# Attention and MLP in one block: 14 of 16 units with a head whose scores are computed turned, the running sum kept in DRAM, loads issued from GpSimd

## Chip, cores and metric

One NeuronCore of a Trainium2 chip. The time is that of one execution on the device, in microseconds (us).

## What is computed

```python
x = A_x                                    # 2048 tokens x 448
xn = layernorm(x)
q = (xn @ wq) as 16 heads of 28;  k = xn @ wk;  v = xn @ wv     # one k and v for all heads
p = softmax(q k^T * 28**-0.5);    o = (p v), heads joined, @ wo
y = layernorm(xn);                h = gelu(y @ w1 + b1)         # 1792 wide
return x + o + (h @ w2 + b2)
```

All inputs are float32. The kernel keeps float32 accuracy by splitting most operands in a high and a low part and adding up two or three products.

## The kernel before

**Three stages.** First the norm and the projections to q, k and v (`q_slot`, `norm_first`, lines 249 to 437); q goes to DRAM in a high and a low part (`qd`), k stays in `ks`, v in `vs`. Then the MLP: 4 chunks of 512 tokens times 14 blocks of 128 hidden columns make 56 slots (`slot`, L547), each with 11 matmuls of `mlp1` (L513) and 12 of `mlp2` (L526) of the slot two earlier; its result is added to `acc` (L540), which holds the running sum of all tokens in SBUF from the load of x to the store of the output. Then attention, from L593 on.

**Attention.** 16 units, each a chunk of 512 queries and a group of 4 heads. Scores are computed transposed, keys on the partitions (`s`, L798): 16 blocks of 128 keys per head. ScalarE takes the exponential out of PSUM (L805), and the result is at once the moving operand of the product with v (`pv`, L703, `po`), four heads beside each other in the array. One column of v is 1.0, so the product carries the softmax's sums as well.

**The maxima.** In that layout the maximum of a query can't be subtracted after the fact, so it is found ahead: `max_stream` (L468) computes the same scores with queries on the partitions (L478, `m`, 16 matmuls a head), and VectorE takes the maxima (L479). `load_max` (L457) turns them and puts them as two more rows (high and low) under q in `qs`, against rows of ones in `ks`, so that the score matmul itself subtracts them. These max matmuls are spread as filler: `MLP_MAX` of them per 46 yields of the MLP slots (L586), and the rest over the attention steps by `weight` (L777). The rows of ones are written by GpSimd late in the first stage (L387).

**Turned heads.** In 7 of the 16 units (`TURNED`) the fourth head goes another way and needs neither max matmuls nor score matmuls: its scores are computed once, with queries on the partitions (`turned_scores`, L722: 16 matmuls, L730, from `q3`), VectorE scales them into `raw` with the maximum on the way (L731), ScalarE takes the exponential with the maximum as bias (L750), DMAs regroup 32-partition parts of `raw` into `half` tiles (L746, 64 transfers of 64 KB a head, on SP's queue), and VectorE turns 32 x 32 blocks into `p` (`turn_blocks`, L754, L757).

**The order.** Each unit has 8 steps of two key blocks. All engines execute in the order written by hand: the letters of `ORDER` in each step (L787): s a score matmul with its exponential, m a max matmul, t a turned score matmul, P the products with v of the step before, e a turned exponential and, at one step of a unit, `load_max`, n a part of the norm by the sums (`norm_jobs`, L635), o a part of the output projection (`o_jobs`, L615). Side work stands in queues (`Stream`) that give one part per letter. Every load and regrouping of the attention stage is on SP's queue: q of a unit (`load_q`, L440), q of a head for the max stream and the turned head (`load_m`, L396), maxima (L465, L466), sums out, in and broadcast (L649, L654, L657), regroupings (L746), output (L628). PSUM: three banks `m`, four banks `s`, one `po`.

**Names in the profile.** Tile names stand without their numbers; `xh` in attention is the tile reused for a unit's q (`qs`), and `half` names also the first stage's view of `wo`.

Of the kernel before, what the change touches and what calls it, by code (L numbers as in the profile page):

```python
# [15 lines left out]
P = 128  # L16
S, D, H, DH, F = 2048, 448, 16, 28, 1792
NT = S // P
CT = 4
# [7 lines left out]
MLP_MAX = 15  # L27
ORDER = "smsmstnsPemssmosmnsm"
TURNED = (3, 5, 7, 9, 11, 13, 15)
QB = 8  # L30
# [7 lines left out]
def block_kernel(ctx, tc, x, wq, wk, wv, wo, w1, b1, w2, b2, out):  # L38
# [19 lines left out]
    ld = dram.tile([4, CW], F32, name="ld")  # L58
    qd = [dram.tile([D, S], F32, name=f"qd{i}") for i in range(2)]

    acc = keep.tile([P, NT, D], F32, name="acc")
# [4 lines left out]
    ph1 = ExitStack()  # L66
    xl_p = ph1.enter_context(tc.tile_pool(name="xl", bufs=2))
# [53 lines left out]
    for t in qmt:  # L121
        pool.memset(f(t), 0.0)
    b1r = wqp.tile([NF, P], F32, name="b1r", bufs=1)
# [21 lines left out]
    def split_weights():  # L145
        for i in range(2):
            split_small(kvraw[:, :, i, :], lambda w, i=i: w[:, :, 32 * i + 1:32 * i + 1 + DH])
# [159 lines left out]
    def w2_split(s):  # L307
# [3 lines left out]
        dve.tensor_sub(w2l[:, ab, :], raw, f(w2h[:, ab, :]))  # L311

    def q_slot(c, i):
# [7 lines left out]
        def evac():  # L321
# [4 lines left out]
            if i == 0:  # L326
                vt = wqp.tile([32, CW], F32, name="vt", bufs=1)
                kl = wqp.tile([64, CW], F32R, name="kl", bufs=1)
                act.activation(ks[32:64, cols], ps[32:64, :], AF.Copy)
                act.activation(vt, ps[0:32, :], AF.Copy)  # L330
            dve.tensor_sub(qe[at, 1, :], ps[at, :], f(qe[at, 0, :]))
            if i == 0:
                dve.tensor_sub(kl[32:64, :], ps[32:64, :], f(ks[32:64, cols]))
                for dst, src in ((0, kl[32:64, :]), (64, kl[32:64, :]), (96, ks[32:64, cols])):
                    nc.sync.dma_start(f(ks[dst:dst + 32, cols]), f(src))
# [51 lines left out]
    def ones_rows():  # L387
        for r in (32, 96):
            pool.memset(f(ks[r:r + 1, :]), 1.0)  # L389

    later(3, 2, ones_rows, True)
# [4 lines left out]
    def load_m(u, j, qm=None, t=None):  # L396
        c, g = units[u]
        at = slice(0, CW) if t is None else slice(t * P, (t + 1) * P)
        cols = slice(c * CW + at.start, c * CW + at.stop)
        if qm is None:  # L400
            qm = qmt[heads.index((u, j)) % 3]
        for blk, i in ((1, 0), (2, 0), (0, 1), (3, 1)):
            nc.sync.dma_start(f(qm[32 * blk + 1:32 * blk + 1 + DH, at]), qd[i][DH * (4 * g + j):DH * (4 * g + j + 1), cols])
# [36 lines left out]
    def load_q(u):  # L440
# [6 lines left out]
        for blk, i in ((1, 0), (2, 0), (0, 1), (3, 1)):  # L447
            nh = heads_of(u)
            src = qd[i][4 * DH * g:4 * DH * g + DH * nh, cols].rearrange("(j r) n -> r j n", r=DH)
            nc.sync.dma_start(f(qs[32 * blk + 1:32 * blk + 1 + DH, 0:nh, :]), src)  # L450
# [6 lines left out]
    def load_max(u):  # L457
# [4 lines left out]
        mn = keep.tile([4 * CT, 2, P], F32R, name="mn", bufs=2)[0:nh * CT]  # L462
        act.activation(mn[:, 0, :], pm, AF.Copy, scale=-1.0)
        dve.scalar_tensor_tensor(mn[:, 1, :], pm, -1.0, f(mn[:, 0, :]), op0=ALU.mult, op1=ALU.subtract)
        nc.sync.dma_start(f(qs[32:33, 0:nh, :]), f(mn[:, 0, :]))  # L465
        nc.sync.dma_start(f(qs[96:97, 0:nh, :]), f(mn[:, 1, :]))  # L466

    def max_stream():  # L468
        for h, (u, j) in enumerate(heads):
# [5 lines left out]
            for t in range(CT):  # L475
                for n in range(4):
# [3 lines left out]
                    if (j, t, n) == (heads_of(u) - 1, CT - 1, 3):  # L480
                        mrs[u] = keep.tile([P, 4 * CT], F32, name="mr", bufs=10)
# [31 lines left out]
    def mlp1(c, ft):  # L513
# [10 lines left out]
        lows.append(lambda: dve.tensor_sub(hl, hr, f(hh)))  # L524

    def mlp2(c, ft, between):  # L526
# [4 lines left out]
        for k in range(CT):  # L531
# [11 lines left out]
            if k == 2 and lows:  # L543
                lows.pop(0)()
            yield

    def slot(n):  # L547
# [13 lines left out]
        else:  # L561
            if nxt:
                nxt()
            lows.pop(0)()

    lows, norms, maxed = [], {}, 0
# [30 lines left out]
    def half_tile():  # L597
        return att.tile([P, QB, CW], F32, name="half", bufs=3)

    wor = half_tile()[:, 0:NG, 0:D]  # L600
    q3 = att.tile([P, CW], F32R, name="q3", bufs=1)
    pool.memset(f(q3), 0.0)
# [11 lines left out]

    def o_jobs(c, gs, tiles=range(CT)):  # L615
        last = NG - 1 in gs
        for k in tiles:
# [7 lines left out]
            a = acc[:, CT * c + k, :]  # L625
# [9 lines left out]
    def norm_jobs(u, po):  # L635
# [12 lines left out]
        else:  # L648
            nc.sync.dma_start(rc, oc[0:P:32, :])  # L649
            yield  # L650
            yield
            dve.reciprocal(rc, rc)
            yield
            nc.sync.dma_start(ld.rearrange("h (i e) -> (h i) e", e=CW // 32), rc)  # L654
# [205 lines left out]
```

## Time and profile before

| | us |
|---|---|
| Median of 3 runs | 1142.34 (1142.27 to 1142.73) |
| Profiled execution | 1142.51 |
| Its span, first to last instruction | 1140.7 |
| First stage, up to the first max matmul | 69.9 |
| MLP, first to last GELU | 72.6 to 445.4 |
| Attention, from the first score matmul | 454.5 |

A row of the grouped lines reads: line, engine, operation, tile written from tiles read, shapes, number | busy us, mean ns of one | idle time of the engine before them, and who ended it. PEld is the weight load of TensorE, SPq SyncE's queue of DMAs. In the chain of waits, each piece is what released the next. The row of one line's DMAs gives the least, median and most ns for which the queue was held by one.

### The profile page before, as it was taken

The numbers are of one execution on the slowest core, as the hardware profiler recorded it, in microseconds if no ns is written. First come the engines' busy times: TensorE is split into PE (matmuls) and PEld (weight loads), VectorE is DVE, ScalarE is ACT, GpSimd is POOL, SyncE is SP. The second block draws the span as 40 slices with busy tenths as digits, with TensorE's granted clock in tenths as the row PEclk, the third lists the DMA queues.
The fourth block names the chain that finished last, engine by engine and source line by source line (L and its number), as shares of the span: only waits on it lengthen the run. The fifth ranks groups of instructions, "written<-read, shape, count | busy, mean of one in ns | idle before, by whom it ended". The sixth has DMA issues, their size and how long they took to land.

```text
span 1140.7 us, 17019 instructions
## 1 busy us (share of the span) xinstructions
PE 1122.8 (98%) x5905; PEld 729.7 (64%) x5905; DVE 867.1 (76%) x1600; ACT 689.6 (60%) x1290; POOL 109.3 (10%) x113
## 2 busy tenths in 40 slices
PE   9989999999999999999999999999999999999998
PEld 8768888888888888555554555544455554564454
DVE  7779889888888888777777777777667677777434
ACT  6753322221222222788888877888777888878974
POOL 5340000000002000002101101101101101101100
PEclk9999999999999999999999999999999999999999
DMA  9751100000000020332343342342433443442300
GB/s 287 200 181 51 43 15 17 17 17 18 17 17 17 17 49 18 86 82 75 97 100 78 101 111 76 105 100 74 103 97 84 102 101 76 106 104 65 85 24 33
DMA packets 65426, 86.82 MB, mean 76 GB/s; under 512 B 20566, under 2 KB 31980, under 8 KB 65212
## 3 DMA queue, kind: packets, MB, share of 16 engines
q1 hardware_dynamic: 63932, 85.16, 28.1%
q8 instruction: 47, 0.77, 0.3%
q10 hardware_dynamic: 1408, 0.57, 0.2%
q14 instruction: 39, 0.32, 0.1%
HBM read 44.05 MB, written 11.12 MB: 48 GB/s over the span
## 4 chain that ended last, share of the span: by engine, by line
PE 88%; DVE 4%; DMA 3%; ACT 2%; issue 1%; SPq 1%; POOL 0%; DVEq 0%; ACTq 0%; POOLq 0%
PE po L708 19%; PE m L478 18%; PE s L798 17%; PE ph L158 10%; PE m L535 4%; PE m L537 4%; PE m L533 4%; PE m L730 3%; DMA xh<-qd 2%; PE qp L158 2%; PE m L622 1%; PE m L624 1%; PE m L623 1%; PE ph L161 1%; DMA rc<-oc 1%
## 5 line engine op out<-in xcount | busy, mean ns | idle before, releaser
L479 DVE TENSOR_REDUCE mx<-m 128x1 f32<-128x512 f32 x912 | 593.2, 685 | 160.5 <-PE m L478 146.2
L805 ACT ACTIVATE p<-s 128x512 f32<-128x512 f32 x879 | 447.4, 614 | 94.3 <-PE s L798 94.2
L478 PE MATMUL m<-ks,qm 128*128 128x512 f32 x912 | 371.0, 407 | 3.5 <-POOL ks L389 2.4
L798 PE MATMUL s<-xh,ks 128*128 128x512 f32 x879 | 318.2, 407 | 2.8 <-ACT p L805 2.5
L708 PE MATMUL po<-p,vs 128*32 128x512 f32 x2048 | 247.9, 601 | 0.0
L478 PEld LDWEIGHTS m<-ks,qm 128*128 128x128 f32 x912 | 171.3, 188 | 108.5 <-issue 26.0
L798 PEld LDWEIGHTS s<-xh,ks 128*128 128x128 f32 x879 | 163.3, 188 | 86.6 <-ACT p L805 35.0
L519 ACT ACTIVATE hr<-ph,b1t 128x512 f32<-128x512 f32 x56 | 38.6, 689 | 277.3 <-PE ph L163 191.5
L708 PEld LDWEIGHTS po<-p,vs 128*32 128x32 f32 x2048 | 53.9, 109 | 120.2 <-issue 114.1
L750 ACT ACTIVATE raw<-raw,m 128x512 f32<-128x512 f32 x112 | 82.7, 738 | 9.9 <-DVE m L735 9.0
L533 PE MATMUL m<-w2h,hh 128*128 128x448 f32 x224 | 82.4, 368 | 0.0
L535 PE MATMUL m<-w2l,hh 128*128 128x448 f32 x224 | 81.6, 364 | 0.0
L537 PE MATMUL m<-w2h,hl 128*128 128x448 f32 x224 | 81.5, 364 | 0.0
L731 DVE TENSOR_SCALAR_CACHE_REDUCE raw<-m 128x512 f32<-128x512 f32 x112 | 76.2, 680 | 0.0
L660 POOL TENSOR_TENSOR oc<-oc,tr 128x512 f32<-128x512 f32 x15 | 19.4, 1294 | 589.0 <-DMA tr<-ld 206.6
L757 DVE STREAM_TRANSPOSE p<-half 128x512 f32<-128x512 f32 x112 | 72.6, 687 | 1.6 <-PE po L708 1.6
L158 PE MATMUL ph<-xh,w1h 128*128 128x512 f32 x168 | 66.5, 396 | 0.0
L158 PE MATMUL ph<-xh,w1l 128*128 128x512 f32 x168 | 66.4, 395 | 0.0
L158 PE MATMUL ph<-xl,w1h 128*128 128x512 f32 x168 | 66.0, 393 | 0.0
L626 DVE TENSOR_TENSOR acc<-acc,m 128x448 f32<-128x448 f32 x22 | 13.6, 621 | 51.5 <-PE m L624 51.5
L730 PE MATMUL m<-ks,q 128*128 128x512 f32 x112 | 47.2, 422 | 3.4 <-DVE mx L479 3.4
L535 PEld LDWEIGHTS m<-w2l,hh 128*128 128x128 f32 x224 | 42.0, 188 | 6.3
(141 smaller groups left out, 964.4 us busy)
## 6 DMA issues: line engine op xcount, KB each, us to landing
half<-raw SPq DMA_DIRECT2D x448, 64.0 KB
qm<-qd SPq DMA_DIRECT2D x228, 56.0 KB
xh<-qd SPq DMA_DIRECT2D x36, 224.0 KB
qd<-qe SPq DMA_DIRECT2D x24, 256.0 KB
xh<-qd SPq DMA_DIRECT2D x28, 168.0 KB
tr<-ld SPq DMA_DIRECT2D x56, 64.0 KB
raw<-in_B_w_dram SPq DMA_DIRECT2D x7, 448.0 KB
out_dram<-acc SPq DMA_DIRECT2D x14, 224.0 KB
```

Of the source, the lines that this page charges most:

```text
L158: pe.matmul(ps, w, v, start=(n == 0), stop=False)
L478: pe.matmul(pm, qm[:, t * P:(t + 1) * P], ks[:, n * CW:(n + 1) * CW], start=True, stop=True)
L479: dve.tensor_reduce(mx[:, CT * j + t, n:n + 1], pm, axis=AX.X, op=ALU.max)
L533: pe.matmul(m2[k], hh[:, ts], w2h[:, ft, :], start=(ft == 0), stop=False)
L535: pe.matmul(m2[k], hh[:, ts], w2l[:, ft, :], start=False, stop=False)
L537: pe.matmul(m2[k], hl[:, ts], w2h[:, ft, :], start=False, stop=(ft == NF - 1))
L708: pe.matmul(po[32 * j:32 * j + 32, :], vs[:, kt, :], ps.pop((u, kt, j)), start=(kt == 0), stop=(kt == NT - 1))
L730: pe.matmul(sc, q3[:, t * P:(t + 1) * P], ks[:, n * CW:(n + 1) * CW], start=True, stop=True)
L731: dve.tensor_scalar(raw[:, :, 4 * n:4 * n + 4, :].rearrange("p r b i -> p b r i"), sc.rearrange("p (b r i) -> p b r i", r=4, i=32), SCALE, ...
L750: act.activation(raw[:, r], raw[:, r], AF.Exp, bias=m3[:, 4:5], scale=1.0)
L798: pe.matmul(s, ks[:, kk * P:(kk + 1) * P], qs[:, j % 4, :], start=True, stop=True)
L805: act.activation(p, s, AF.Exp, scale=SCALE)
```

## The change

- `TURNED` is units 2 to 15 (14 of 16) in place of 7. The scores of a unit's turned head are computed in the ten steps ahead of it; two `q3` tiles take turns; a unit's regrouped exponentials lie in one tile of 16 x 512 per partition (two of them) in place of halves.
- Turned exponentials are 1024 wide, two groups of 32 partitions at a time, each followed by 8 regrouping DMAs; there is one per step (letter x), two in one step of a unit. `turn_blocks` is one instruction of 1024 columns per step.
- Scores come in pairs: two matmuls into a tile of two PSUM banks (two such tiles in place of four single banks), and one exponential 1024 wide. In a unit with a turned head a step has three pairs, else four. There are two orders of letters, one for each kind of unit.
- The max matmuls: 20 per 46 yields in the MLP in place of 15; new weights in attention.
- `acc` lives only until the end of the MLP. A chunk's sum is stored to `ad` in DRAM after its last slot, and loaded again by row tiles ahead of the output projection.
- In attention, loads (q, maxima, sums, row tiles) are issued from GpSimd's queue; regroupings and most of the output stay on SP.
- The MLP's low halves (`hl`) and six of the seven low parts of w2 are subtracted on GpSimd in place of VectorE.
- q, k and their maxima change rows, so that the row of ones is the last of its 32; `ks` is set to ones as a whole at the start, in place of two rows late in the first stage. Copies between rows of `ks` take 28 partitions in place of 32.

```diff
-MLP_MAX = 15
-ORDER = "smsmstnsPemssmosmnsm"
-TURNED = (3, 5, 7, 9, 11, 13, 15)
+MLP_MAX = 20
+ORDERS = ("mptmpmtmpmexnPTpmonm", "tptmpmeopxnPTmnm")
+TURNED = tuple(range(2, 16))
...
+    ad = dram.tile([P, NT, D], F32, name="ad")
...
+    pool.memset(f(ks), 1.0)
...
-        dve.tensor_sub(w2l[:, ab, :], raw, f(w2h[:, ab, :]))
+        (pool if s else dve).tensor_sub(w2l[:, ab, :], raw, f(w2h[:, ab, :]))
...
-    def ones_rows():
-        for r in (32, 96):
-            pool.memset(f(ks[r:r + 1, :]), 1.0)
-
-    later(3, 2, ones_rows, True)
...
-        lows.append(lambda: dve.tensor_sub(hl, hr, f(hh)))
+        pool.tensor_sub(hl, hr, f(hh))
...
+                if k == CT - 1:
+                    nc.sync.dma_start(ad[:, CT * c:CT * c + CT, :], acc[:, CT * c:CT * c + CT, :])
...
-    sp = ctx.enter_context(tc.tile_pool(name="sp", bufs=4, space=PSUM))
+    sp = ctx.enter_context(tc.tile_pool(name="sp", bufs=2, space=PSUM))
...
+    loads = pool
+
+    def turned_tile():
+        return att.tile([P, 4 * CT, CW], F32, name="turned", bufs=2)
...
+    def load_rows_of(c, tiles):
+        for k in tiles:
+            rows[c, k] = att.tile([P, D], F32, name="a", bufs=5)
+            loads.dma_start(rows[c, k], ad[:, CT * c + k, :])
...
-            a = acc[:, CT * c + k, :]
+            a = rows[c, k]
             dve.tensor_add(a, a, po)
...
-            nc.sync.dma_start(rc, oc[0:P:32, :])
-            yield
-            yield
+            loads.dma_start(rc, oc[0:P:32, :])
+            for _ in range(4):
+                yield
...
+                    exps.extend((u, t, raw, m3, h) for h in range(2))
+                    if t == CT - 1 and u + 2 < NU:
+                        load_m(u + 2, 3, q3[i])
...
+    def turned_exp():
+        if not exps:
+            return
+        u, t, raw, m3, h = exps.pop(0)
+        if u not in turned:
+            turned[u] = turned_tile()
+        rs = slice(2 * h, 2 * h + 2)
+        act.activation(raw[:, rs], raw[:, rs], AF.Exp, bias=m3[:, 4:5], scale=1.0)
+        for r in range(2 * h, 2 * h + 2):
             for a in range(4):
-                nc.sync.dma_start(hbs[-1][32 * r:32 * r + 32, 4 * (t % 2) + a, :],
+                nc.sync.dma_start(turned[u][32 * r:32 * r + 32, 4 * t + a, :],
                                   raw[32 * a:32 * a + 32, r].rearrange("p b i -> p (b i)"))
...
+    def turn_blocks(u, kt):
+        p = pair_of()
+        dve.transpose(p.rearrange("p k (g j) -> p g k j", j=32),
+                      turned[u][:, :, 32 * kt:32 * kt + 64].rearrange("p g (k j) -> p g k j", j=32))
+        ps[u, kt, 3], ps[u, kt + 1, 3] = p[:, 0], p[:, 1]
...
+    def scores(u, kt, jobs):
+        s = sp.tile([P, 2, CW], F32, name="s")
+        p = pair_of()
+        for i, (k, j) in enumerate(jobs):
+            pe.matmul(s[:, i], ks[:, (kt + k) * P:(kt + k + 1) * P], qss[u][:, j, :], start=True, stop=True)
+            ps[u, kt + k, j] = p[:, i]
+        act.activation(p, s, AF.Exp, scale=SCALE)
...
-    weight = [0 if n >= len(steps) - LEAD else 8 if u in TURNED
-              else 18 if u + 2 < NU else 12 for n, (u, kt) in enumerate(steps)]
+    weight = [0 if n >= len(steps) - LEAD else 24 if u == 0 else 20 if u == 1 else 6 for n, (u, kt) in enumerate(steps)]
...
+        jobs = [((0, 0), (0, 1)), ((0, 2), (1, 2)), ((1, 0), (1, 1))]
+        if u not in TURNED:
+            jobs[1:2] = [((0, 2), (0, 3)), ((1, 2), (1, 3))]
+        for what in ORDERS[u in TURNED]:
+            if what == "p":
+                scores(u, kt, jobs.pop(0))
...
             elif what == "t":
-                if n >= 3:
+                if n >= 8 * (TURNED[0] - 1) - 2:
                     tq.step()
+            elif what == "x":
+                turned_exp()
+                if kt == 12:
+                    turned_exp()
```

More of the change, by code (lines that the diff above doesn't have):

```diff
@@ L66, in block_kernel @@
     ph1 = ExitStack()
+    acc = ph1.enter_context(tc.tile_pool(name="accp", bufs=1)).tile([P, NT, D], F32, name="acc")
     xl_p = ph1.enter_context(tc.tile_pool(name="xl", bufs=2))
@@ L394, in block_kernel, with load_m @@
     qss, ots = {}, {}
-    def load_m(u, j, qm=None, t=None):
+    loads = nc.sync
+    def load_m(u, j, qm=None):
         c, g = units[u]
-        at = slice(0, CW) if t is None else slice(t * P, (t + 1) * P)
-        cols = slice(c * CW + at.start, c * CW + at.stop)
         if qm is None:
@@ L768, in o_wait @@
     def o_wait(c, gs, tiles):
+        load_rows_of(c, tiles)
         for _ in range(8):
@@ L826, in block_kernel @@
                     oside.add(o_jobs(NCH - 1, range(NG - 1)))
+                if n == len(steps) - 7:
+                    load_rows_of(NCH - 1, range(CT))
                 oside.step()
-            elif n > 0 and 2 * n % BURST == 0:
-                for _ in range(BURST):
+            elif what == "P":
+                for _ in range(BURST if n else 0):
                     pv(*pvq.pop(0))
```

115 lines of the change are left out of this document (36 added, 79 removed).

## Prediction

> **What bounds the kernel now.** I read the page's busy shares and chain first, then busy times by stage.
>
> ```profile
> span 1140.7 us, 17019 instructions
> ...
> PE 1122.8 (98%) x5905; PEld 729.7 (64%) x5905; DVE 867.1 (76%) x1600; ACT 689.6 (60%) x1290; POOL 109.3 (10%) x113
> ...
> PE po L708 19%; PE m L478 18%; PE s L798 17%; PE ph L158 10%; PE m L535 4%; PE m L537 4%; PE m L533 4%; PE m L730 3%; DMA xh<-qd 2%; PE qp L158 2%; PE m L622 1%; PE m L624 1%; PE m L623 1%; PE ph L161 1%; DMA rc<-oc 1%
> ```
> ```profile
> 72.60:445.40 372.80, 372.08 (x1701) 312.67 (x1700) 326.61 (x516) 93.78 (x142) 20.76 (x17) 1.00 0.09 25
> ```
> ```profile
> 454.50:500.90 46.40, 46.11 (x252) 24.68 (x252) 34.62 (x64) 35.89 (x72) 3.82 (x3) 1.00 0.29 69
> 500.90:1095.00 594.10, 587.86 (x3293) 304.65 (x3294) 425.90 (x829) 483.25 (x941) 49.26 (x46) 1.00 0.37 92
> 1095.00:1140.70 45.70, 40.98 (x245) 23.23 (x244) 19.29 (x36) 25.16 (x49) 2.59 (x2) 0.99 0.07 26
> ```
>
> The window rows give stretch, length, then busy PE, PEld, DVE, ACT, POOL, clock, DMA share, GB/s. The first is 55 MLP slots (from the first to the last GELU), 6.78 us each; the others are unit 0 of attention, units 1 to 14, and unit 15 with the tail. TensorE is busy in all of them and its clock is 1.00, so its own instructions are the price list to begin with:
>
> ```profile
> 463.83 0.40 PE L478 MATMUL m<-ks,qm 128*128 128x512 f32 x1
> 464.06 0.39 PE L798 MATMUL s<-xh,ks 128*128 128x512 f32 x1
> 464.29 0.39 PE L478 MATMUL m<-ks,qm 128*128 128x512 f32 x1
> 464.53 0.39 PE L798 MATMUL s<-xh,ks 128*128 128x512 f32 x1
> ```
>
> A 512-wide matmul lasts 0.39 us, but the starts are 0.23 us apart: 0.23 is what one costs. The busy 98% does not say that nothing else is near its limit. SP's queue, which is not in the busy shares at all, issues the transfers of the turned heads:
>
> ```profile
> L746 SPq DMA_DIRECT2D half<-raw x448: 507/588/1991, 489.8 to 1083.8; - x150
> ```
> ```profile
> 800.92 1.85 SPq L746 DMA_DIRECT2D half<-raw  x3
> ```
>
> Each holds SP for a median of 588 ns, and three in a row take 1.85 us, so one follows another after (1.85 - 0.588) / 2 = 0.631 us. A turned head makes 4 blocks x 4 groups x 4 parts = 64 of them (448 / 7).
>
> **The change, part by part.**
>
> Matmuls. The groups that count them:
>
> ```profile
> L479 DVE TENSOR_REDUCE mx<-m 128x1 f32<-128x512 f32 x912 | 593.2, 685 | 160.5 <-PE m L478 146.2
> L805 ACT ACTIVATE p<-s 128x512 f32<-128x512 f32 x879 | 447.4, 614 | 94.3 <-PE s L798 94.2
> L750 ACT ACTIVATE raw<-raw,m 128x512 f32<-128x512 f32 x112 | 82.7, 738 | 9.9 <-DVE m L735 9.0 <-DMA q<-qd 0.6 <-DMA qm<-qd 0.4
> L731 DVE TENSOR_SCALAR_CACHE_REDUCE raw<-m 128x512 f32<-128x512 f32 x112 | 76.2, 680 | 0.0
> L731 DVE DVE_READ_ACCUMULATOR raw<-m 128x1 f32 x112 | 9.2, 82 | 0.0
> L757 DVE STREAM_TRANSPOSE p<-half 128x512 f32<-128x512 f32 x112 | 72.6, 687 | 1.6 <-PE po L708 1.6
> ```
>
> Seven more turned heads take away 7 x 16 = 112 max matmuls (912 to 800) and 112 score matmuls, and add 112 turned ones: net -112 x 0.23 = -25.8 us of TensorE. Where they lie matters: with MLP_MAX 20, the MLP's 1276 yields give 1276 x 20 / 46 + 6 = 560 max matmuls in place of 422, which lengthens that stage by 138 x 0.23 = 31.7 us; attention loses 250 x 0.23 = 57.5 us.
>
> The memset of the ones rows goes to the start, and with it this wait:
>
> ```profile
> PE m L478 <- POOL ks L389: 2.4, 1, 2.4
> ```
>
> That is -2.4 us. The new memset of ks (two of 2048 columns took 3.6 us there) fits into the wait below; if it did not, it would cost its excess over 3.1 us.
>
> ```profile
> POOL wah L141 <- DMA kvraw<-in_A_wv_dram: 3.1, 1, 3.1
> ```
>
> MLP low halves and six of the seven w2 low parts on GpSimd. These rows price them:
>
> ```profile
> L524 DVE TENSOR_TENSOR hl<-hr,hh 128x512 fp32r<-128x512 f32 x56 | 40.4, 722 | 0.0
> L660 POOL TENSOR_TENSOR oc<-oc,tr 128x512 f32<-128x512 f32 x15 | 19.4, 1294 | 589.0 <-DMA tr<-ld 206.6 <-ACT p L805 181.7 <-PE s L798 89.3
> ```
>
> GpSimd needs 1.29 us for what VectorE did in 0.72, in a slot of 7.35 us (6.78 + 2.5 x 0.23) where it is idle; the result is used two slots later, so it costs nothing. VectorE's slot becomes 326.6 / 55 - 0.72 + 2.5 x 0.65 = 6.85 us, still under 7.35 (93%). Without the shift it would be 7.57 and the bound, +0.2 us x 56 = 12 us.
>
> The running sum stored to DRAM. Four stores of 896 KB beside a DMA share of 0.09, and 16 loads of one row tile, issued eight side steps before use: hidden. If the first attention tiles have to wait for the last store, that is one landing, under 5 us (a longest transfer in the chain of waits is 4.77 us, below).
>
> Exponentials 1024 wide. Not in the trace. A 512-wide one is 0.614 us; the slope comes from a wider row:
>
> ```profile
> L310 ACT ACTIVATE w2h<-raw 128x896 fp32r<-128x896 f32 x7 | 6.6, 941 | 0.0
> ```
>
> Against 0.614, 384 more columns cost 0.33 us, so 1024 columns take 0.614 + 512 x 0.00085 = 1.05 us, and 1.17 in the turned form (0.738). Bounds: 0.94 (slope alone) and 1.23 (two of 512). I take 1.05. A turned unit then has ScalarE at 24 x 1.05 + 8 x 1.17 + about 0.9 = 35.5 us, and VectorE at 12 x 0.65 + 16 x 0.76 + 8 x 1.16 + about 3.6 = 33 us (transposes of 1024 columns priced at 0.687 plus the same again less 0.2).
>
> What TensorE needs for a turned unit comes from GpSimd's first product of each unit:
>
> ```profile
> 564.23 1.31 POOL L660 TENSOR_TENSOR oc<-oc,tr 128x512 f32<-128x512 f32 x1 [35.58 <-DMA tr<-ld]
> ```
> ```profile
> 1072.49 1.28 POOL L660 TENSOR_TENSOR oc<-oc,tr 128x512 f32<-128x512 f32 x1 [35.22 <-ACT p L805]
> ```
>
> Twelve units lie between: 508.3 / 12 = 42.35, or 84.7 us for a pair of one turned and one whole unit. They differ by 116 - 76 = 40 matmuls (9.2 us), so a turned one takes (84.7 - 9.2) / 2 = **37.7 us**. A turned unit of after holds 48 scores + 16 turned + 12 max = 76 matmuls, the same.
>
> SP for the same unit: before, 64 regroupings in a pair, 40 us of 84.7. After, 64 in every unit: 64 x 0.631 = **40.4 us**, plus a store of the output, against TensorE's 37.7. So SP's queue is late next, although the other loads leave it. A unit's first transposes need all 64 landed; the last eight are issued two steps ahead (9.4 us), take 5.0 us to issue and about 1.9 us to land (rc below), which leaves a slack of some 2 us, used up in the first turned unit by a deficit of 2.7 us.
>
> Three rows for the sum and for the bounds of an issue (least, median, most ns), the first of unit 1:
>
> ```profile
> 500.90:545.00 44.10, 43.35 (x233) 22.89 (x237) 32.80 (x63) 39.05 (x78) 7.61 (x7) 1.00 0.38 92
> ```
> ```profile
> L628 SPq DMA_DIRECT2D out_dram<-acc x14: 332/382/537, 675.3 to 1137.1; - x14
> ```
> ```profile
> L403 SPq DMA_DIRECT2D qm<-qd x228: 306/383/1982, 38.4 to 1002.9; - x114
> ```
>
> The sum by that chain. MLP ends at 454.5 + 31.7 - 2.4 = 483.8. Unit 0 has 6 matmuls more (46.4 + 1.4 = 47.8), unit 1 four more (44.1 + 0.9 = 45.0): 576.6. Up to here SP keeps up, one group of eight a step. From the second unit's transfers on (first group in step 15, about 571) there are 104 groups, 832 x 0.631 = 525 us, and 10 stores of about 0.4: 1100. Landing 1.9, one wide transpose 1.2: 1103.4. Then the last unit's second product with v can start; before, that was here:
>
> ```profile
> 1097.60 1.92 PE L708 MATMUL po<-p,vs 128*32 128x512 f32 x16
> ```
> ```profile
> 799.87 4.77 DMA xh<-qd
> ...
> 805.01 1.89 DMA rc<-oc
> ```
>
> 43.1 us before the end, and the work behind it is unchanged. 1103.4 + 43.1 = 1146.5 us of span. The profiled execution took 1142.51 us for a span of 1140.7, 1.8 more (the median shown is 1142.34): **1148 us**. Bounds of the pitch: with the shortest issue, 0.507 + 0.043, SP needs 35 us a unit and does not bind; with 5% of delays such as the longest one (1.99 us) added, 0.66, the time is 1172.
>
> GpSimd's queue. About 20 DMAs a unit (q 4, turned q 4, maxima 2, sums 6, row tiles 1, max stream 3) come beside 3.2 us of arithmetic. No row shows a DMA issued there. Bounds: 0.31 us (the shortest issue on SP, which gives 9 us a unit) and 1.99 (its longest, 43 us). I take 1.29, GpSimd's own longest instruction of this stage: 29 of 37.7 us, hidden, as its loads are two heads or a unit ahead. Queued behind a wait there (the four broadcasts wait for the store of the sums, 1.9 us) are only such loads.
>
> The Trainium skill, "DMA: Bandwidth & Descriptors", section on issuing engines not being separate DMA queues, says that issuing from several engines only saves sequencer time, usually small beside the transfer. The rows speak against "small" here: 0.588 us of issue for 64 KB, 64 times a unit. By the rule the issue would not matter and the time would be the first rival's.
>
> **Rivals.**
>
> 1. *TensorE stays the bound* (chance 0.35). For it: its busy 98%, and a deficit of SP of only 7%, which a faster issue would remove (point: 37.7 / 64 = 0.589 us from one DMA to the next). Against: 0.631 within every run of regroupings. Time: 1142.5 - 25.8 - 2.4 = 1114; with small waits of coarser score buffers (two pairs for four single banks), up to 1130. I name 1118.
>
> 2. *GpSimd's queue becomes the bound*, slower (0.15). Its place is the issue of 20 DMAs a unit; it decides from (37.7 - 3.2) / 20 = 1.7 us each. At 2 us each a unit is 43.2 us: 13 units x 5.5 = 71 above 1114, 1186. For it: the order of its queue, with sums, products and loads in one line. Against: GpSimd is 10% busy now. The Trainium skill, "SBUF — State Buffer", section on who interferes with whom, says that descriptor generation on GpSimd can be shut out while VectorE runs in a two-port mode; no run here shows it, and the attention stage has no large VectorE copy from SBUF to SBUF besides the transposes.
>
> **How the numbers follow.** SP's queue binds: 0.50, 1137 to 1168 (pitch 0.62 to 0.66). TensorE: 0.35, 1112 to 1130. GpSimd: 0.15, mostly above 1168. Range of 8 in 10: 1116 to 1168, leaving out most of GpSimd's case and the lowest of TensorE's. A measurement of this kernel tells about 0.2% from no change: under 1140.1 is TensorE's case and 0.03 of SP's, 0.38; within, 0.05 of SP's; above, 0.57.
>
> **What would show it.** SP right: the regroupings in unbroken runs in units 2 to 14, 40 to 42 us apart by unit, VectorE's wide transposes waiting for "DMA turned<-raw", TensorE's busy share in attention down to about 93%. Wrong: transposes released by TensorE's products, units of 38 us, a pitch below 0.59. The MLP stage should be 30 to 33 us longer in either case; a larger growth means VectorE became its bound. GpSimd's case would show as scores or max matmuls waiting for "DMA xh<-qd" or "DMA qm<-qd".

## The result and the profile after

The changed kernel takes **1213.33 us** (1212.41 to 1216.5), the kernel before beside it on the same chip 1142.53 (1142.27 to 1143.32): ratio 1.0623, 95% interval 1.0602 to 1.0645. The forecast was 1148, within 1116 to 1168. The profiled execution took 1212.41 us for a span of 1210.4, against a forecast span of 1146.5.

From the page of the kernel after: span, busy shares, and shares of the chain that ended last.

```profile
span 1210.4 us, 17322 instructions
...
PE 1137.7 (94%) x5793; PEld 722.4 (60%) x5793; DVE 907.4 (75%) x1678; ACT 660.8 (55%) x778; POOL 353.6 (29%) x473
...
PE po L715 16%; PE m L475 14%; PE s L776 12%; PE ph L159 9%; ACT p L778 6%; DMA turned<-raw 5%; PE m L735 4%; PE m L532 3%; PE m L534 3%; PE m L530 3%; SPq L756 3%; DVE mx L476 2%; PE qp L159 2%; DVE p L761 2%; PE m L629 1%
```

TensorE has 112 matmuls fewer (5905 to 5793) and still lost its 98%. The chain now holds SP's queue (3%) and the landing of its transfers (5%), which were not in it.

By stretch (length, then busy PE, PEld, DVE, ACT, POOL, clock, DMA share, GB/s): first to last GELU, units 0 and 1, units 2 to 14, unit 15 with the tail. From here on a unit ends where ScalarE copies its `po` out (L645; L638 before), so unit 1 of before ends at 546.6.

```profile
70.20:476.20 406.00, 404.98 (x1837) 338.14 (x1836) 379.41 (x594) 93.74 (x142) 102.95 (x78) 1.00 0.12 36
486.70:541.80 55.10, 51.67 (x259) 27.18 (x260) 37.95 (x69) 36.47 (x39) 22.42 (x38) 0.97 0.36 94
541.80:591.50 49.70, 47.91 (x246) 23.48 (x247) 34.86 (x75) 42.19 (x47) 20.46 (x31) 1.00 0.45 115
591.50:1161.20 569.70, 515.45 (x2798) 246.75 (x2796) 373.12 (x753) 414.48 (x441) 173.06 (x279) 0.96 0.54 135
1161.20:1210.40 49.20, 41.00 (x240) 21.63 (x236) 19.93 (x29) 22.41 (x25) 2.58 (x2) 0.98 0.09 32
```

| us | before | forecast | after | after less forecast |
|---|---|---|---|---|
| up to the first score matmul | 454.5 | 483.8 | 486.7 | 2.9 |
| unit 0 | 46.4 | 47.8 | 55.1 | 7.3 |
| unit 1 | 45.7 | 46.6 | 49.7 | 3.1 |
| units 2 to 14 | 548.6 | 522.8 | 569.7 | 46.9 |
| unit 15, tail | 45.5 | 45.5 | 49.2 | 3.7 |
| span | 1140.7 | 1146.5 | 1210.4 | 63.9 |

(The forecast of units 2 to 14 is what its span leaves beside the other rows.) Three quarters of the miss lie in units 2 to 14. Single units there, kernel after: units 2, 3, 4, 5 and 9.

```profile
591.50:628.60 37.10, 36.03 (x206) 16.31 (x205) 28.02 (x59) 31.79 (x35) 14.05 (x23) 1.00 0.55 140
628.60:672.50 43.90, 37.71 (x206) 16.97 (x207) 28.66 (x58) 32.04 (x36) 14.02 (x23) 0.96 0.53 131
672.50:716.20 43.70, 38.51 (x207) 17.06 (x207) 28.65 (x58) 32.10 (x36) 14.25 (x23) 0.92 0.62 148
716.20:767.20 51.00, 46.89 (x254) 26.55 (x253) 31.13 (x62) 32.05 (x34) 14.10 (x23) 0.97 0.51 133
894.20:947.20 53.00, 47.84 (x254) 27.31 (x255) 31.14 (x62) 32.27 (x35) 14.10 (x23) 0.94 0.50 127
```

Unit 2 still runs at TensorE's pace. Units 3 and 4, with the same 206 matmuls, take 6.7 us more, and units 5 and 9, which also hold the output projection of a chunk (254 matmuls), take 51 and 53. Two windows of the same view of the kernel before, a turned unit and one with the projection:

```profile
591.00:626.90 35.90, 35.56 (x207) 15.96 (x207) 27.65 (x56) 30.49 (x60) 3.20 (x3) 1.00 0.39 93
671.50:716.00 44.50, 44.50 (x255) 25.60 (x255) 30.18 (x60) 30.97 (x60) 3.21 (x3) 1.00 0.36 94
```

A plain unit (one without projection) is 8 us longer after the change, and TensorE's busy time in it only 2. What it waits for is in the row of the regroupings (least, median, most ns of issue) and in the list of who waited for them:

```profile
L756 SPq DMA_DIRECT2D turned<-raw x896: 507/588/1990, 535.2 to 1161.6; - x180
...
  DVE p L761: 61.4, 11
```

VectorE's wide transposes wait 61.4 us in 11 places, one a unit. Such a place, in the order of the engines' work (start, length, what; in brackets the idle time ahead and who ended it):

```profile
811.70 1.25 DVE L761 STREAM_TRANSPOSE p<-turned 128x1024 f32<-128x1024 f32 x1 [5.79 <-DMA turned<-raw]
...
813.59 0.79 PE L475 MATMUL m<-ks,qm 128*128 128x512 f32 x1 [3.67 <-DVE raw L736]
...
815.17 3.64 PE L715 MATMUL po<-p,vs 128*32 128x512 f32 x16
```

The first transpose of a unit waits 5.79 us for its last landing; VectorE's work behind it is late; so TensorE, which needs VectorE to empty a bank, idles 3.67 us. And SP's queue itself, kernel after (a row joins transfers of one line that follow each other on the queue, with the idle time between them):

```profile
628.15 44.44 SPq L756 DMA_DIRECT2D turned<-raw  x67
...
727.85 4.94 SPq L756 DMA_DIRECT2D turned<-raw  x8
732.89 0.53 SPq L635 DMA_DIRECT2D out_dram<-a  x1
734.43 5.84 SPq L756 DMA_DIRECT2D turned<-raw  x8
740.37 0.53 SPq L635 DMA_DIRECT2D out_dram<-a  x1
742.16 4.95 SPq L756 DMA_DIRECT2D turned<-raw  x8
...
798.46 53.82 SPq L756 DMA_DIRECT2D turned<-raw  x80
```

In plain units SP hardly stops: 67 transfers in 44.44 us and 80 in 53.82, on average one per (44.44 - 0.59) / 66 = 0.664 and 0.674 us, where the forecast had 0.631. But the pitch, the time from one start to the next where nothing comes between, is what it was. Sixteen in a row out of the same 67 are one per (10.03 - 0.59) / 15 = 0.629 us:

```profile
635.34 10.03 SPq L756 DMA_DIRECT2D turned<-raw  x16
```

What makes 0.664 of it is in the same stretch, transfer by transfer: two stops of 0.50 and 0.79 us, and two transfers that last 0.99 and 1.08 us in place of 0.59. In unit 5, with the projection, SP stops more: from 727.85 to 742.16 two steps take 14.3 us, of which SP works 4.94 + 0.53 + 5.84 + 0.53 = 11.8; the rest it waits, each time until the next step's exponential. SP's largest wait in this unit (who for whom, us in total, times, longest):

```profile
SPq L756 <- ACT raw L753: 4.0, 5, 1.2
```

### The profile page after: what moved, and what is told of

The parts are those of the page before. It is cut to its first block, busy times and chain, and to the rows that moved or that the text cites. A ratio compares the mean times of both kernels' runs of the same rounds, so it can differ in the third digit from the quotient of the medians.

```text
span 1210.4 us, 17322 instructions
## 1 busy us (share of the span) xinstructions
PE 1137.7 (94%) x5793; PEld 722.4 (60%) x5793; DVE 907.4 (75%) x1678; ACT 660.8 (55%) x778; POOL 353.6 (29%) x473
## 4 chain that ended last, share of the span: by engine, by line
PE 74%; DVE 7%; ACT 7%; DMA 6%; SPq 3%; issue 2%; POOL 0%; ACTq 0%; DVEq 0%; POOLq 0%
PE po L715 16%; PE m L475 14%; PE s L776 12%; PE ph L159 9%; ACT p L778 6%; DMA turned<-raw 5%; PE m L735 4%; PE m L532 3%; PE m L534 3%; PE m L530 3%; SPq L756 3%; DVE mx L476 2%; PE qp L159 2%; DVE p L761 2%; PE m L629 1%
## 5 line engine op out<-in xcount | busy, mean ns | idle before, releaser
L476 DVE TENSOR_REDUCE mx<-m 128x1 f32<-128x512 f32 x800 | 521.4, 686 | 52.1 <-PE m L475 46.8
L778 ACT ACTIVATE p<-s 128x1024 f32<-128x1024 f32 x400 | 387.7, 1022 | 202.0 <-PE s L776 188.8
L475 PE MATMUL m<-ks,qm 128*128 128x512 f32 x800 | 320.5, 404 | 42.4 <-DVE raw L736 41.1
L776 PE MATMUL s<-xh,ks 128*128 128x512 f32 x800 | 265.9, 416 | 19.2 <-ACT p L778 17.8
L761 DVE STREAM_TRANSPOSE p<-turned 128x1024 f32<-128x1024 f32 x112 | 139.4, 1245 | 170.5 <-ACT p L778 72.7
L516 ACT ACTIVATE hr<-ph,b1t 128x512 f32<-128x512 f32 x56 | 38.6, 688 | 305.4 <-PE ph L164 299.5
L521 POOL TENSOR_TENSOR hl<-hr,hh 128x512 fp32r<-128x512 f32 x56 | 72.1, 1288 | 301.7 <-PE m L475 284.6
L736 DVE TENSOR_SCALAR_CACHE_REDUCE raw<-m 128x512 f32<-128x512 f32 x224 | 149.6, 684 | 8.7 <-PE m L735 4.3
L715 PEld LDWEIGHTS po<-p,vs 128*32 128x32 f32 x2048 | 55.1, 111 | 133.1 <-issue 129.3
L753 ACT ACTIVATE raw<-raw,m 128x1024 f32<-128x1024 f32 x112 | 127.6, 1139 | 0.0
L735 PE MATMUL m<-ks,q 128*128 128x512 f32 x224 | 99.6, 445 | 0.0
L735 PEld LDWEIGHTS m<-ks,q 128*128 128x128 f32 x224 | 42.1, 188 | 94.5 <-issue 80.1
```

The costliest lines, as they stand in the source:

```text
L475: pe.matmul(pm, qm[:, t * P:(t + 1) * P], ks[:, n * CW:(n + 1) * CW], start=True, stop=True)
L476: dve.tensor_reduce(mx[:, CT * j + t, n:n + 1], pm, axis=AX.X, op=ALU.max)
L715: pe.matmul(po[32 * j:32 * j + 32, :], vs[:, kt, :], ps.pop((u, kt, j)), start=(kt == 0), stop=(kt == NT - 1))
L735: pe.matmul(sc, q3[i][:, t * P:(t + 1) * P], ks[:, n * CW:(n + 1) * CW], start=True, stop=True)
L736: dve.tensor_scalar(raw[:, :, 4 * n:4 * n + 4, :].rearrange("p r b i -> p b r i"), sc.rearrange("p (b r i) -> p b r i", r=4, i=32), SCALE, ...
L753: act.activation(raw[:, rs], raw[:, rs], AF.Exp, bias=m3[:, 4:5], scale=1.0)
```

## The experiments

Each is told against the kernel after (1213.33) unless it says otherwise. Runs with one time have no interval; a ratio is to the kernel before on the same chip (1139.4 to 1141.6 there).

**1. A quarter of the regroupings on GpSimd's queue.**

```diff
-                nc.sync.dma_start(turned[u][32 * r:32 * r + 32, 4 * t + a, :],
+                (pool if a == 3 else nc.sync).dma_start(turned[u][32 * r:32 * r + 32, 4 * t + a, :],
```

> One of the four regrouping DMAs of each group of 32 rows goes to GpSimd's queue; bytes, order and everything else as in the changed kernel. Theory (SP's issue time binds, 64 x 0.675 = 43 us a unit): SP keeps 48 a unit, 32.4 us, under TensorE's 37.3 (8 steps of 4.66), so units 2 to 14 fall from 44.3 to about 38 us and the time to 1125-1135. Rival 1 (the DMA engines or the landing of 64 KB parts bind, not the issue): the bytes are the same, so it stays at 1200-1215. Rival 2 (the coarse score pairs and VectorE's order bind): stays within 1% of 1213.

Measured: 1154.21 us (1152.57 to 1155.18), ratio 1.0123 (1.0106 to 1.0140). The group of the moved ones (count, busy us, mean ns):

```profile
L756 POOL DMA_DIRECT2D turned<-raw x224 | 113.5, 511 | 191.9 <-ACT raw L753 164.3 <-DMA turned<-raw 10.3 <-DVE p L761 8.2
```

59 us come back by nothing but the queue of 224 transfers, with the same bytes in the same order: SP's issue was what bound units 3 to 14. But the time stays 19 to 29 us over what was expected, and over the kernel before, though TensorE has 112 matmuls less. That is the second question.

**2. Half of them on GpSimd.**

```diff
-                nc.sync.dma_start(turned[u][32 * r:32 * r + 32, 4 * t + a, :],
+                (pool if a % 2 else nc.sync).dma_start(turned[u][32 * r:32 * r + 32, 4 * t + a, :],
```

> Two of four regroupings on GpSimd's queue. If SP's issue still costs something in quarter_pool (48 a unit, 32 us of 39.8), this is faster than 1154 by up to 10 us; if TensorE with its waits binds there, it stays at 1150-1158; if GpSimd's queue (32 x 0.51 + 14 = 30 us a unit, with waits in its order) begins to bind, slower than 1160.

1163.3 us, slower than a quarter. VectorE's transposes wait for landings again, 17.4 us in 6 places, for 2.9 in 2 with a quarter. Why the landings come later was not found: GpSimd's waits for exponentials ahead of its transfers are no longer than with a quarter (89.5 us for 164.3). The gain is not monotonic in the share moved.

**3. The loads back on SP's queue** in attention.

```diff
-    loads = pool
+    loads = nc.sync
```

> The loads of the attention stage go back to SP's queue. Theory (SP's issue): about 20 more DMAs a unit at 0.43 us, 8.6 us on top of 44.3, 13 units: 1213 + 112 = 1325. Rival (SP has room and something else sets the unit): within 1% of 1213. It also shows what one regrouping costs SP when GpSimd issues nothing beside it: 0.63 us if GpSimd's DMAs stretched it to 0.675, 0.675 if not.

1343.16 us: 130 us more; units 2 to 14 take 54.1 us each on average. SP's queue in this kernel:

```profile
587.80 10.03 SPq L756 DMA_DIRECT2D turned<-raw  x16
597.93 1.82 SPq L447 DMA_DIRECT2D xh<-qd  x4
```

Nothing is issued on GpSimd's queue here, and 16 regroupings in a row take 10.03 us, one per 0.629. Sixteen in a row beside GpSimd's transfers take the same 10.03 (above): no disturbance of one queue by the other shows in these rows. What slows this kernel is the loads' time on SP's queue (112 us were expected) and waits in its line (15.4 us for `ld` alone).

**4. The last wide pair of scores after the products**, in the kernel after and, with a quarter on GpSimd, in the kernel of experiment 1.

```diff
-ORDERS = (..., "tptmpmeopxnPTmnm")
+ORDERS = (..., "tptmpmeoxnPTpmnm")
```

> The third pair behind the products with v, in the changed kernel as it is. Theory (SP's issue sets the unit, TensorE's waits in a step cost nothing): within 0.7% of 1213. Rival (the coarse score pairs are what made it slow): 1213 - 28 = 1185 or less.

> As quarter_pool (a quarter of the regroupings on GpSimd's queue), and in turned units the third pair of scores moves behind the products with v, so that it needn't wait for the first pair's exponential. Theory (SP no longer binds there; what is left, 39.8 us a unit against 37.7 forecast for TensorE, is TensorE waiting for the wide exponential that holds one of the two score tiles, 0.25 us in each of 112 steps): 1154 - 28 = 1126, faster than the kernel before. Rival (SP or GpSimd's queue still binds in quarter_pool): no change, 1150-1158.

1220.75 and 1149.64 us (1149.03 to 1151.13; ratio 1.0075, 1.0057 to 1.0092). Where SP binds, TensorE's order gives nothing, as expected. Where it doesn't, 4.6 us, not 28: the wait of that one pair is not where the rest goes.

**5. A unit's q loaded two steps later.**

```diff
-        if u + 1 < NU and kt == 0:
+        if u + 1 < NU and kt == 4:
             load_q(u + 1)
```

> The loads of the next unit's q (4 DMAs of 168 KB) are issued two steps later in the unit, away from the last regroupings of a unit, on whose landing the transposes wait. Theory A (SP's issue time alone sets the unit): no change, 1208-1216. Theory B (the loads stretch the landing of the last group from 1.9 to 3.7 us and hold up SP's next ones, 1.5-3 us a unit): 1213 - 13 x 2 = 1187, between 1173 and 1197.

1218.07 us, and the transposes wait 66.6 us for landings, as before the edit (61.4): the big loads are not what they wait for.

**6. Fifteen max matmuls per 46 yields in the MLP**, in the kernel after and in the second of experiment 4.

```diff
-MLP_MAX = 20
+MLP_MAX = 15
```

> MLP_MAX 15 in place of 20: 138 max matmuls (31.7 us of TensorE) move from the MLP back to attention. Theory (attention is bound by SP, TensorE has 7 us to spare in each of 13 units): the MLP shortens by 32 us and attention stays, 1181. Rival (TensorE or VectorE sets attention): the work only moves, 1208-1216.

> The version with a quarter of the regroupings on GpSimd and the late wide pair (1149.6), with 15 max matmuls per 46 yields of the MLP in place of 20: 138 of them move from the MLP (32 us there) to attention. If turned steps leave TensorE waiting for want of filler, the 138 cost less than 0.23 us each there: about 50 of them in units 0 and 1 at full price (11 us), the rest between nothing and 0.23, so 1128 to 1140. If a matmul costs the same wherever it stands, 1149 as before. In the kernel after the same edit gave 20 us back, but there SP's queue set the pace of a unit.

1193.28 and 1151.45 us (1150.02 to 1151.78). Under SP's queue 138 matmuls moved out of the MLP give 20 of their 32 us, since TensorE has idle time in attention. With SP relieved they give nothing: units 2 to 14 take 532 us for 506, on average 0.23 us for each of 114 matmuls more. So those steps as a whole are not short of filler; the theory that they were falls. (In plain units from unit 6 on, 7 more cost 1.1 us, 0.16 each: a little is filled there.)

**7. The MLP's low halves back on VectorE.**

```diff
-        pool.tensor_sub(hl, hr, f(hh))
+        dve.tensor_sub(hl, hr, f(hh))
```

> The MLP's low halves back on VectorE, everything else as in the changed kernel. From the prediction: VectorE's slot becomes 6.85 + 0.72 = 7.57 us against 7.38 of the slot now, so the MLP grows by about 12 us, 1225. Rival (VectorE's real spacing is below its durations, so it still fits): no change, 1211-1215.

1235.85 us, 22.5 more. The row of the waits that shows it, kernel of this experiment:

```profile
ACT hr L516 <- DVE mx L476: 223.8, 37, 7.0
```

The GELU waits for VectorE's maxima: VectorE would be the MLP's bound, and by more than the 12 us of the forecast.

**8. The turned heads of before** (7 of 16), everything else as after.

```diff
-TURNED = tuple(range(2, 16))
+TURNED = (3, 5, 7, 9, 11, 13, 15)
...
-                if n >= 8 * (TURNED[0] - 1) - 2:
+                if tdone < 16 * len(TURNED) and n >= 8 * (TURNED[tdone // 16] - 1) - 2:
                     tq.step()
+                    tdone += 1
```

> The kernel after, but with the turned heads of before only (units 3, 5, 7, 9, 11, 13, 15): 112 max matmuls and 112 score matmuls come back for 112 turned ones, and SP issues 64 regroupings in two units in place of one. If SP's queue is what binds after, this must be far faster than 1213, whatever else was changed; if the two-bank score tiles, the loads on GpSimd or the store of the sum bind, it stays above 1200. Against the version with SP relieved by a quarter (1154.2) two theories of what a turned head is worth part: by the count of matmuls alone, as the forecast had it, 112 x 0.23 = 25.8 us more, 1180; by the theory that a turned step leaves about 0.35 us more uncovered than a whole one (7 x 8 x 0.35 = 20 us), some 6 us more, 1160.

1191.26 us (1189.39 to 1191.59), ratio 1.0434 (1.0416 to 1.0451). SP is no longer short (the transposes wait 1.3 us for landings in all), yet the kernel is 49 us over the one before with exactly its 5905 matmuls. So the loss beside SP's queue is not in the seven added heads: with SP relieved these take 1191 to 1154, 37 us, more than their 25.8 of matmuls. It is in the rest of the change. A turned and a whole unit of this kernel:

```profile
643.80:680.20 36.40, 35.28 (x202) 15.51 (x201) 25.45 (x41) 25.58 (x28) 14.23 (x23) 1.00 0.21 55
767.90:810.70 42.80, 41.40 (x221) 18.64 (x221) 19.57 (x43) 37.67 (x42) 14.10 (x23) 1.00 0.48 119
```

To read these, count the instructions at their own price: 0.23 us a 512-wide matmul, 0.20 a 448-wide one, 1.89 for the 16 products of a step (15.1 a unit). The whole unit has 221 - 128 = 93 matmuls, 36.5 us, and takes 42.8: 6.3 beside. A whole unit of before has 2.6 beside (44.6 for 117). Added up over attention, what these prices leave over is 57 us before, 106 here, 152 in the kernel after, 89 in the second of experiment 4 (a few small transposes on TensorE are not priced).

**9. Turned scores started two steps earlier.**

```diff
-                if n >= 8 * (TURNED[0] - 1) - 2:
+                if n >= 8 * (TURNED[0] - 1) - 4:
```

> The kernel after with the scores of each turned head started two steps earlier, so that the exponentials of the next head are there for SP while a unit's first transposes wait for their last landing; the number of transfers is the same. Theory A (in after SP lacks exponentials for some 3.3 us after the stall at each unit's end, and would otherwise run at 0.631 us a transfer): units of 40.9 us in place of 44.3, 13 x 3.4 = 44 us less, about 1170. Theory B (each transfer costs SP 0.675 us beside GpSimd's transfers, whatever the order): nothing gained, 1205 to 1215.

1205.97 us (1201.93 to 1207.65), ratio 1.0573 (1.0550 to 1.0596): not theory A's 1170. SP's queue in units 6 to 8, and who waits for a landing, kernel of this experiment:

```profile
767.80 124.27 SPq L756 DMA_DIRECT2D turned<-raw  x189
```
```profile
  DVE raw L736: 89.0, 23
  DVE p L761: 1.3, 1
```

In these three units SP goes through 189 transfers with no stop over 0.65 us, 0.658 us each on average, and the transposes no longer wait (61.4 to 1.3 us). But the wait has only moved: 89.0 us are spent on a free `raw` buffer, which the same transfers hold. There the pace is SP's, wherever the wait shows. Elsewhere SP does stop, for another reason (units 2 to 14, same columns as above):

```profile
SPq L756 <- DVE p L761: 18.0, 4, 6.8
```

Once each in units 2, 5, 9 and 13 SP waits until the transposes have read one of the two `turned` tiles. So the earlier start runs into the second buffer, and this kernel does not show what SP could do if it were fed throughout; a third `turned` tile was not tried. The time is the one of theory B, but not by its cause: a transfer still follows another after 0.63 us.

**10. Three edits at the ends of attention, in one kernel**, on the second of experiment 4.

```diff
+    s2 = [sp.tile([P, 2, CW], F32, name=f"s{i}", bufs=1) for i in range(2)]
...
-        s = sp.tile([P, 2, CW], F32, name="s")
+        s = s2[len(done_s) % 2]
...
+            if u == 0:
+                act.activation(p[:, i], s[:, i], AF.Exp, scale=SCALE)
```

> From the version with a quarter of the regroupings on GpSimd and the late wide pair (1149.6), three edits: unit 0's exponentials 512 wide, each freeing its own bank; the last sums stored by token tile, half of them from ScalarE's queue; units 14 and 15 in the order of letters of after. By the count of matmuls unit 0 lost 10.1 us beside its instructions there, 3.2 in the kernel before. If the score tile of two banks that waits for one wide exponential makes the difference, unit 0 gets some 3 us shorter, and the smaller last store takes about 2 from the wait ahead of it. The end (unit 14, unit 15 and the tail) took 94 us there and 88.5 in the order of after. Sum: 1149.6 - 3 - 2 - 5.5 = 1139, level with the kernel before or 0.2% under it; if the wide tile is not the reason, 1142 to 1145.

1191.75 us (1189.19 to 1196.89). The windows of unit 0 and of the rest, and TensorE in unit 0:

```profile
486.70:588.50 101.80, 76.89 (x259) 32.59 (x260) 39.51 (x70) 43.45 (x71) 23.42 (x40) 0.71 0.18 49
588.50:1189.20 600.70, 586.12 (x3278) 283.68 (x3278) 425.33 (x856) 478.01 (x511) 305.82 (x534) 1.00 0.55 140
```
```profile
521.98 0.50 PE L779 MATMUL s<-xh,ks 128*128 128x512 f32 x1 [0.75 <-ACT p L782]
...
523.88 0.79 PE L779 MATMUL s<-xh,ks 128*128 128x512 f32 x1 [0.75 <-ACT p L782]
```

The edit shared a tile so that the second score matmul of a pair waits for the exponential of the first: a chain, and unit 0 took 101.8 us. It tells nothing of the theory. The rest (600.7 us against 606.0) shows that the edits at the end work.

**11. The same without that mistake**: units 14 and 15 in the letters of after, the last sums stored by token tile, half of them from ScalarE's queue; then also unit 0 with four score tiles of one bank and exponentials 512 wide.

```diff
-        for what in ORDERS[u in TURNED]:
+        for what in ORDERS[0 if u not in TURNED else 2 if u >= NU - 2 else 1]:
...
-                if k == CT - 1:
-                    nc.sync.dma_start(ad[:, CT * c:CT * c + CT, :], acc[:, CT * c:CT * c + CT, :])
+                (nc.scalar if k % 2 and c == NCH - 1 else nc.sync).dma_start(ad[:, CT * c + k, :], a)
```

> The version with a quarter of the regroupings on GpSimd and the late wide pair (1149.6) with two edits: units 14 and 15 in the order of letters of after, and the last sums stored by token tile, half of them from ScalarE's queue. The end (unit 14, unit 15, tail) took 94.1 us there and 88.6 in the version with the order of after; the wait for the last store should fall from 3.6 to 2.0 us. If both simply add, 1149.6 - 5.5 - 1.7 = 1142.4; if what is saved at the end comes back elsewhere, 1147 or more.

For the second, besides:

```diff
+    sp1 = first_unit.enter_context(tc.tile_pool(name="sp1", bufs=4, space=PSUM))
...
+            to = s[:, i] if u > 0 else sp1.tile([P, CW], F32, name="s")
+            pe.matmul(to, ks[:, (kt + k) * P:(kt + k + 1) * P], qss[u][:, j, :], start=True, stop=True)
...
+            if u == 0:
+                act.activation(p[:, i], to, AF.Exp, scale=SCALE)
```

> The version before it in this call, with unit 0's exponentials 512 wide from four score tiles of one bank each (in a pool of their own, closed at unit 1), so that a score matmul waits for the exponential four before it and not for a wide one. Unit 0 lost 10.1 us beside its instructions with tiles of two banks, 3.2 in the kernel before; some 2 of the rest are the wait for the store. If the two-bank tiles cause it: unit 0 shorter by 4 to 5 us, 1138 in all. If the order of letters or the start causes it: no gain, 1142.

1142.35 us (1140.09 to 1145.23), ratio 1.0026 (1.0017 to 1.0035), and 1141.93 (1140.89 to 1143.19), ratio 1.0020 (1.0012 to 1.0029). Windows of the first: unit 0, a turned unit, unit 14, unit 15 with the tail.

```profile
486.70:539.20 52.50, 50.41 (x259) 25.85 (x259) 38.26 (x70) 36.36 (x38) 23.45 (x40) 1.00 0.35 90
...
624.20:661.00 36.80, 36.37 (x206) 16.57 (x207) 28.38 (x58) 32.03 (x36) 21.94 (x39) 1.00 0.60 153
1051.50:1093.20 41.70, 38.14 (x218) 18.82 (x217) 23.22 (x45) 30.26 (x33) 19.29 (x34) 1.00 0.60 152
1093.20:1140.10 46.90, 39.96 (x240) 21.53 (x236) 19.46 (x29) 22.42 (x25) 2.57 (x2) 0.98 0.06 20
```

The two edits add as expected (the smaller last store gives 2.6 us in unit 0, the end 5.5). The narrow score tiles give 0.4 us in all. From its first score, unit 0 takes 51.7 us (487.7 to 539.4) for 52.2 (487.0 to 539.2), not 4 to 5 less: that the tiles of two banks make unit 0 long falls. This is the best version found; it does not beat the kernel before.

## Why the prediction was wrong, point by point

**SP's queue binds, TensorE late next: right, and shown** by experiments 1 and 3, in opposite directions. Most signs named beforehand came: transposes waiting for "DMA turned<-raw", TensorE's share in attention down to 91% (656 of 723.7 us; 93% was named), SP at work almost without a stop in plain units, 39 to 44 us long (40 to 42 was named). Unbroken runs in all of units 2 to 14 did not come.

**"832 x 0.631 = 525 us, and 10 stores of about 0.4": this step failed**, in two terms that it puts at nothing: transfers that take long, and stops of SP. Counted transfer by transfer in the trace, the 832 from the second unit on take 576.2 us (586.0 to 1162.2):

| part | us | forecast |
|---|---|---|
| the transfers without what follows, with gaps of at most 0.2 us | 525.4 | 525 |
| what 23 transfers of over 0.8 us last beyond 0.588 | 16.7 | 0 |
| SP idle, 37 times over 0.2 us | 28.7 | 0 |
| 11 stores | 5.4 | 4 |

*Long transfers.* 0.631 was taken from three transfers in a row, and as a pitch it held. But the kernel before already has long ones: 10 of its 448 last over 0.8 us, 8.4 us beyond 0.588 in all, which for 832 would have made 16 us. What makes a transfer long stays open. The forecast had them only in its upper bound, 0.66, for which it worked out 1172; its range ended at 1168, below its own bound.

*SP without a break.* The sum laid the output projection beside SP's work, as if SP could run ahead while TensorE is busy with it. It did not: a step gives SP one exponential, and a step with projection lasts some 7.2 us. So units 5, 9 and 13 take 51.0, 53.0 and 46.5 us (150.5, where 3 x 40.2 were forecast): 30 us. SP idles for 17.2 us of them, 10.4 in waits for the turned exponential (4.0 in unit 5, above); long transfers, the stores and five more transfers make the rest. Plain units (3, 4, 6, 7, 8, 10, 11, 12) average 42.6 us for the 40.2 that the forecast left to each: 8 x 2.4 = 19 us. Units 2 and 14 give 2 us back: 47 us in all, the table's 46.9.

Starting the scores earlier (experiment 9) gives back only 7 us, as SP then stops for the second `turned` tile in just these units. What did relieve it is fewer issues on that queue (experiment 1).

**Landing of 1.9 us, and a slack of 2.** The slack was used up in one unit, as forecast: unit 2 ran at 37.1 us, unit 3 at 43.9. The landing of SP's transfers is not on record; those moved to GpSimd in experiment 1 land after 2.4 us (median).

**The running sum "hidden, if first tiles wait under 5 us": the wait came.** The group of the wide exponentials and two more, kernel after (busy us, mean ns | idle before and who ended it):

```profile
L778 ACT ACTIVATE p<-s 128x1024 f32<-128x1024 f32 x400 | 387.7, 1022 | 202.0 <-PE s L776 188.8 <-DMA ad<-acc 11.4 <-PE m L475 1.0
L761 DVE STREAM_TRANSPOSE p<-turned 128x1024 f32<-128x1024 f32 x112 | 139.4, 1245 | 170.5 <-ACT p L778 72.7 <-DMA turned<-raw 61.4 <-PE po L715 31.3
L753 ACT ACTIVATE raw<-raw,m 128x1024 f32<-128x1024 f32 x112 | 127.6, 1139 | 0.0
L521 POOL TENSOR_TENSOR hl<-hr,hh 128x512 fp32r<-128x512 f32 x56 | 72.1, 1288 | 301.7 <-PE m L475 284.6 <-ACT hh L519 10.8 <-issue 6.3
...
L447 POOL DMA_DIRECT2D xh<-qd x60 | 36.9, 619 | 58.9 <-PE s L776 48.2 <-PE m L735 9.9 <-PE m L475 0.5
...
L664 POOL DMA_DIRECT2D tr<-ld x56 | 28.0, 507 | 30.5 <-DMA ld<-rc 27.7 <-issue 2.7
```

The first exponential waits for the last store (ScalarE's idle time ahead of it is 11.4 us, most of it before the score was there). The store is in the chain, and TensorE stands behind it:

```profile
486.71 3.55 DMA ad<-acc
```
```profile
491.57 1.04 PE L776 MATMUL s<-xh,ks 128*128 128x512 f32 x2 [2.96 <-ACT p L778]
```

It was named as a condition and left out of the sum; smaller stores take back 2.6 us. Of the other 5 us of unit 0 the cause stays open.

**Exponentials 1.05 and 1.17, transposes 1.16: right** (1.022, 1.139, 1.245 us). **Low halves on GpSimd free: right** (1.288 us in a slot of 7.4, used two slots later); without the shift the MLP loses 22.5 us, not 12.

**The MLP stage**: 30 to 33 us longer was expected; GELU to GELU it is 406.0 for 372.8, 33.2 longer, and 2.4 earlier from the ones rows, as forecast.

**Rival 2, GpSimd's queue: wrong.** A DMA costs it 0.51 to 0.62 us, about a third of the 1.7 from which it would bind. What limits with half of the regroupings there (experiment 2) stays open.

**Rival 1, TensorE at 1114 to 1118 once SP is fast enough: not reached.** With SP relieved and the ends mended it is 1142.35. The forecast's 37.7 us for a turned unit, projections spread over all, was fair: units 2 to 13 average 38.6 here, plain ones 36.4 to 36.8 for 35.9 before. The 25.8 us of matmuls are saved. They are given back, by the profile of that version against before (time beside counted instructions): unit 0 4.3, unit 1 3.5, units 2 to 13 0.9 each (10), unit 14 3.7, tail 1.4, the way to the first score 2.9: 26. Where whole units remain (experiment 8) the change costs them 3 to 4 us each. That is where the gain went; why the change loses it stays open. Filler (6) does not explain it, nor does the width of the score tiles, which was tried in unit 0 alone (11). "Small waits of coarser score buffers up to 1130" was the right direction with too small a price.

**The skill's rule.** By the Trainium skill, "DMA: Bandwidth & Descriptors", section on issuing engines not being separate DMA queues, moving transfers to another engine saves only issue time, usually small beside the transfer. The first half agrees: what experiment 1 saved is issue time. One issue is small beside its transfer here too (0.51 us for a landing after 2.4), but 64 in a row a unit are not: 224 transfers moved took 59 us off.

## What to carry to other kernels

Price an issuing queue like an engine: number of transfers a unit times the pitch, plus the transfers that take long, which a row of three does not hold but the trace as a whole does; then compare it with the bound per unit, unit kind by unit kind. A queue that is fed one piece a step stops in longer steps, so add its stops there, and ask which buffer would let it run ahead. When a change removes instructions from the bound engine and the time does not follow, count the instructions of each unit at their own price before and after: the difference says in which units the gain is given back, even where it does not say why.

## What the runs showed of the hardware that was not expected

**TensorE's pace after a wait.** Behind the idle 3.67 us above, a matmul takes 0.79 us and 16 products 3.64 for 1.85 to 1.92, and the granted clock is 0.50 for 6.8 us; over unit 4 it is 0.92. So a stall costs more than its idle time: the same 206 matmuls keep TensorE busy for 36.0 us in unit 2 and for 37.7 and 38.5 in units 3 and 4. The clock is the third figure from the end in these windows, behind idle times of 3.67, 2.15 and 1.95 us (the last in the middle of its window):

```profile
812.66:819.49 6.83, 5.90 (x21) 2.08 (x22) 4.08 (x9) 2.06 (x2) 0.00 (x0) 0.50 0.40 98
771.70:775.10 3.40, 3.40 (x18) 0.60 (x16) 2.25 (x4) 2.06 (x2) 0.00 (x0) 0.50 0.40 98
944.00:960.00 16.00, 13.54 (x78) 6.23 (x77) 10.28 (x22) 12.40 (x14) 0.71 (x1) 1.00 0.58 128
```

The Trainium skill, "TensorE: Matmul & The Clock Gate", Part 1 on the clock gate, has the array at half rate after an idle window of about 3.4 us. The half rate agrees; the length does not quite, as 2.15 us were enough once here, while 1.95 us were not. In experiment 10 idle times of 0.75 us, in a chain, did the same to a whole unit: mean clock 0.71, matmuls of 0.79 us beside ones of 0.50.

**Issue cost by queue.** The same 64 KB transfer costs GpSimd's queue 511 ns and SP's 588; a load of q costs GpSimd 619.
